# Retention and a squared-ReLU feed-forward network on one core: w_out loaded in fp32 and cast on chip, and seven products in place of eight for half of the first block

## The chip, the core and the metric

The kernel runs on one core of a Trainium2 chip. The core has a matrix engine (TensorE, PE in the profile, with its weight loads as PEld), three engines for elementwise work (VectorE or DVE, ScalarE or ACT, GpSimd or POOL) and a queue engine (SyncE or SP) that issues transfers between the memory outside and the on-chip memory. Each engine works through its own list of instructions in order and waits on semaphores for the others. TensorE writes into PSUM, in banks of 2 KB a partition, from which ScalarE or VectorE must fetch the results. The metric is the device time of one execution in microseconds; lower is better.

## What is computed

The reference is a linear attention with a decay of its own in each head, followed by a feed-forward network with squared ReLU:

```python
for t in range(S):
    state = gamma[None, :, None, None] * state + np.einsum('bhd,bhe->bhde', k[:, :, t], v[:, :, t])
    y[:, :, t] = scale * np.einsum('bhd,bhde->bhe', q[:, :, t], state)
...
x = np.ascontiguousarray(attn_out.transpose(0, 2, 1, 3)).reshape(B * S, H * D)
h = np.maximum(x @ w_in, 0.0)
return (h * h @ w_out).astype(np.float32)
```

There are 4 batches, 8 heads, 768 positions and a head size of 64, so x has 3072 rows of 512. w_in is 512 x 2048, w_out 2048 x 512. All inputs and the output are fp32; the kernel multiplies in bf16 and sums in fp32.

## The kernel before

The 3072 rows are 24 chunks of 128 tokens. Chunks are put together to blocks: the first block (block 0) has four, the other ten have two each. A chunk goes through the attention (scores within the chunk, a mask, the running state, an output y that is copied to `xt`), and a block then through the network: the first product `x @ w_in`, with the 2048 hidden units in 16 f-blocks of 128; ReLU on ScalarE (line 835) and the square on VectorE (line 806); the second product with w_out.

The order is written out by hand. After a prologue (lines 1052 to 1116) the program is a row of numbered pieces of TensorE work, made by the generator `ffn_pieces`; block 0 covers pieces 5 to 32, block 1 begins at 33. `put(place, ...)` hangs other work (a load, a cast, a part of the attention of a later chunk) behind the piece of that number, and each engine gets its instructions in the order in which the pieces and the hung work are written. `attend(m, ...)` hangs the attention of chunk m on five places: scaled q and k (line 361, VectorE) and the cast of v (line 377, POOL), the transposes with their copies on ScalarE (lines 391 to 411), two halves of scores (line 430) each with a mask on VectorE (line 437), the state (line 458), and the outputs (lines 498 and 506). The scores go through a single PSUM bank, `ps_st`, so the second half needs the first half's mask to be done. The products share four PSUM banks in the pool `ps_f`.

In block 0 pieces 5 to 16 are first products of all 512 rows at once (line 826). Pieces 17 to 32 are the second product (line 1022): for each quarter of w_out (four f-blocks), four chunks in turn, four matmuls of 512 columns each, 64 in all; the four results are copied out by ScalarE (line 1032) and stored.

Blocks 2 to 10 (`SEVEN`) do the second product otherwise. Seen as a product of 2 x 2 blocks (two chunks by even and odd f-blocks, times even and odd f-blocks by the two halves of the columns), it takes seven products of eight matmuls with 256 columns in place of eight products, in the form of Strassen and Winograd. For that VectorE makes four sums of the hidden units (s1 to s4), and once for the whole kernel four sums of w_out (t1 to t4, `sum_w_out`, line 319). Before, these are hung on places 25 (first half, four instructions), 31 (two) and 48 (two).

w_in arrives in fp32 through SP's queue into four staging tiles (pool `stage`, 4 buffers) and is cast to bf16 by VectorE, ScalarE and POOL (lines 329 to 333). w_out arrives through POOL's queue, in four quarters hung on places 6, 8, 11 and 14, and the transfer itself makes bf16 of it:

```python
nc.gpsimd.dma_start(w_out_bf[g][:], w_out_v[:, g * FPQ : (g + 1) * FPQ, :])
```

The staging tiles are used again from place 22 on by loads of k and v for later batches (line 145).

Of the kernel before, what the change touches and what calls it, by code (L numbers as in the profile page):

```python
# [9 lines left out]
FP32 = mybir.dt.float32  # L10
# [3 lines left out]
AF = mybir.ActivationFunctionType  # L14
ALU = mybir.AluOpType
# [16 lines left out]
def kernel(  # L32
# [123 lines left out]
    staged = {}  # L156
# [10 lines left out]
        staged["in", g] = t  # L167

    def load_w_out(g):
        nc.gpsimd.dma_start(w_out_bf[g][:], w_out_v[:, g * FPQ : (g + 1) * FPQ, :])  # L170

    load_q4(0)
    load_pair(0, "kn", k, raw_k, heads_of[0])
# [14 lines left out]
    def exponents(pattern, step, name, logs, parts=(slice(0, P),)):  # L188
# [35 lines left out]
        out=ident[:],  # L224
# [96 lines left out]
    def cast_w(kind, g, halves=(0, 1), on="VVSG"):  # L321

        src = staged[kind, g]
        dst = (w_in_bf if kind == "in" else w_out_bf)[g]
        for half in halves:
            c = slice(half * 256, (half + 1) * 256)
            for j, engine in enumerate(on):
                if engine == "G":
                    nc.gpsimd.tensor_copy(dst[:, j, c], src[:, j, c])
                elif engine == "V":  # L330
                    nc.vector.tensor_copy(dst[:, j, c], src[:, j, c])
                else:
                    nc.scalar.activation(dst[:, j, c], src[:, j, c], AF.Copy)

    idle_ps = []

# [503 lines left out]
    def seven_products(tb):  # L840
# [115 lines left out]

        return first_sums, rest if tb + 1 < len(BLOCKS) else rest_at_end

    open_ps = {}

    def first_unit(tb, g, c, parts=(0, 1)):

        if tb not in h2s:
            h_tiles(tb)
        if (tb, g, c) not in open_ps:
            open_ps[tb, g, c] = ps_f.tile([P, FPQ, C], FP32, name="psf")
        hp = open_ps[tb, g, c]
        cols = slice(c * C, (c + 1) * C)
        half = FPQ // 2
        for part in parts:  # L970
            for fq in range(part * half, (part + 1) * half):
                first_product(tb, hp[:, fq, :], g * FPQ + fq, cols)
        if 1 in parts:
            relu(h_of(tb, g * FPQ, (g + 1) * FPQ)[:, :, cols], open_ps.pop((tb, g, c)))

    def ffn_pieces(tb):
        nch = BLOCKS[tb]
        TB = nch * C
        if tb == 0:
            for f in range(FPQ, NFB):  # L980
                hp = ps_f.tile([P, TB], FP32, name="psf")
                first_product(tb, hp[:], f, slice(0, TB))
                relu(h_of(tb, f)[:, 0], hp)
                yield
        elif tb <= 2:

            for c in range(nch):
                for g in range(NQ):
                    first_unit(tb, g, c)
                    if tb in SEVEN and (c, g) == (1, 3):  # L990
                        first_sums, rest = seven_products(tb)
                        first_sums(slice(0, 4))
                    yield
            if tb in SEVEN:
                yield from rest()
                return
        else:
            h_tiles(tb)
            per = 512 // TB
            if tb in SEVEN:  # L1000
                first_sums, rest = seven_products(tb)
            for f0 in range(0, NFB, per):
                hp = ps_f.tile([P, per, TB], FP32, name="psf")
                for f in range(f0, f0 + per):
                    first_product(tb, hp[:, f - f0, :], f, slice(0, TB))
                relu(h_of(tb, f0, f0 + per), hp, tb in SEVEN and f0 // per in (1, 3))
                if f0 // per in (1, 2, 3) and kept:
                    next(kept[0])
                if f0 // per == 4:
                    kept.clear()  # L1010
                if f0 // per == 5 and tb in SEVEN:
                    first_sums(slice(0, 4))
                yield
            if tb in SEVEN:
                yield from rest()
                return


        def second(op, j, g, cols=slice(0, DM)):
            for fq in range(FPQ):  # L1020
                f = g * FPQ + fq
                nc.tensor.matmul(  # L1022
                    op[:],
                    lhsT=h_of(tb, f)[:, 0, j * C : (j + 1) * C],
                    rhs=w_out_bf[g][:, fq, cols],
                    start=(f == 0),
                    stop=(f == NFB - 1),
                )
# [8 lines left out]
        together = nch if tb == 0 else 1  # L1037
        for j0 in range(0, nch, together):
            ops = [ps_f.tile([P, DM], FP32, name="psf") for _ in range(together)]
            for g in range(NQ):  # L1040
                for j, op in enumerate(ops):
                    second(op, j0 + j, g)
                    if g == NQ - 1:
                        store(op, j0 + j)
                    yield


    tp, st, f = (ps_tp, "tp"), (ps_st, "st"), (ps_f, "psf")
# [75 lines left out]
    def put(place, what, *args):  # L1124
        parts.setdefault(place, []).append((what, args))
# [16 lines left out]
    def attend2(m, d, before, q_at, qturn_at, k_at, turn_at, v_at):  # L1142
# [103 lines left out]
```

## Time and profile before

| | us |
|---|---|
| median of 3 runs (204.67 to 205.03) | 204.86 |
| the profiled execution | 204.37 |
| its span on the engines | 202.5 |
| TensorE busy | 195.7 |
| VectorE busy | 151.2 |
| ScalarE busy | 127.6 |
| POOL busy | 68.0 |
| second product of block 0, first matmul to the first of block 1 | 30.92 to 47.63 |
| w_out's four loads, issue to landing | 7.1 to 13.8 |

The profile shows one execution. Times in it count from the start of the span; the execution's own time is 1.9 us longer than the span. A line of the timeline gives start, duration (of a run of like instructions, from the first's start to the last's end), engine, source line, operation, what is written from what, how many, and in brackets how long the engine stood idle before it and what ended the wait. A matmul's duration includes its way through the array, so the step between starts, not the duration, is what one costs in a row of them.

### The profile page before, as it was taken

Reading aid. Unit: us, or ns where it says so; the run is one execution under the profiler, and the core shown is the slowest. Engines: PE = TensorE matmul, PEld = TensorE weight load, DVE = VectorE, ACT = ScalarE, POOL = GpSimd, SP = SyncE. Lnnn points to the kernel's source line nnn. Section 1 sums busy time; section 2 is a strip of 40 time slices with the busy share of each in tenths; the row PEclk is TensorE's granted clock in tenths of the full one; section 3 lists DMA queues with packets and bytes.
Section 4 is the critical chain, followed back from the end, with each engine's and each line's share of the span. In section 5 each row is a group of like instructions: output and inputs, shape, how many; then the busy total and the mean of one; then the engine's idle time right before and its main releaser. Section 6 shows DMA issues by size and latency. Waiting matters only on the chain.

```text
span 202.5 us, 5744 instructions
## 1 busy us (share of the span) xinstructions
PE 195.7 (97%) x2321; PEld 160.1 (79%) x2327; DVE 151.2 (75%) x309; ACT 127.6 (63%) x258; POOL 68.0 (34%) x131
## 2 busy tenths in 40 slices
PE   5899999999999999999999999999999999999993
PEld 1478444558965998988989999999889899999883
DVE  3986768268597888788798798798797797485374
ACT  8764872348853766782784785783775776763730
POOL 8693711311330552282225225252225225100000
PEclk9999999999999999999999999999999999999999
DMA  5999999999979478979979998979998254300202
GB/s 169 356 375 398 338 195 197 260 233 320 236 160 262 125 159 156 202 204 223 171 214 164 214 208 203 226 182 227 212 157 200 107 105 49 111 3 0 107 0 104
DMA packets 92250, 38.12 MB, mean 188 GB/s; under 512 B 68544, under 2 KB 88256, under 8 KB 92224
## 3 DMA queue, kind: packets, MB, share of 16 engines
q1 hardware_dynamic: 90112, 35.66, 72.3%
q0 software_dynamic: 2112, 2.10, 6.2%
q8 instruction: 18, 0.29, 0.6%
q14 instruction: 8, 0.07, 0.1%
HBM read 27.26 MB, written 6.29 MB: 166 GB/s over the span
## 4 chain that ended last, share of the span: by engine, by line
PE 89%; DVE 4%; DMA 2%; ACT 2%; issue 1%; DVEq 0%
PE psf L826 40%; PE psf L860 18%; PE psf L1022 10%; PE tp L860 7%; DMA qn<-in_q_dram 2%; PE y L783 2%; PE st L727 2%; PE y L776 2%; PE c_ps L754 2%; DVE h L806 1%; PE c_ps L627 1%; PE st L430 1%; PE y L506 1%; ACT h L835 1%; PE y L342 1%
## 5 line engine op out<-in xcount | busy, mean ns | idle before, releaser
L826 PE MATMUL psf<-xt,w_in_bf 128*128 128x256 bf16 (+2 forms) x879 | 92.2, 259 | 0.2 <-issue 0.2
L826 PEld LDWEIGHTS <-w_in_bf 128*128 128x128 bf16 x880 | 71.2, 98 | 11.4
L835 ACT ACTIVATE h<-psf 128x512 bf16<-128x512 f32 x96 | 56.1, 594 | 20.1 <-PE psf L826 18.5
L806 DVE TENSOR_TENSOR h<-h 128x512 bf16<-128x512 bf16 x80 | 35.6, 460 | 19.2 <-ACT h L835 18.8
L688 POOL CAST ks_bdp<-stage 64x512 bf16<-64x512 f32 x32 | 24.5, 767 | 38.7 <-issue 30.7
L705 POOL COPY v_bd<-v 64x512 bf16<-64x512 bf16 x32 | 20.6, 643 | 42.0 <-DVE v L697 36.7
L860 PEld LDWEIGHTS <-h 128*128 128x128 bf16 x288 | 26.3, 98 | 3.8 <-DVE h L806 1.0
L1022 PE MATMUL psf<-w_out_bf,h 128*128 128x512 bf16 x91 | 21.9, 379 | 0.4 <-issue 0.2
L860 PE MATMUL tp<-w_out_bf,h 128*128 128x256 bf16 x136 | 19.4, 273 | 0.2 <-DVE h L806 0.2
L860 PE MATMUL psf<-w_sum,h 128*128 128x256 bf16 x136 | 19.1, 273 | 0.0
L860 PE MATMUL psf<-w_sum,k_bd 128*128 128x256 bf16 x144 | 17.9, 273 | 0.0
L361 DVE TENSOR_TENSOR qs<-qn,qf 128x512 bf16<-128x512 f32 x20 | 16.3, 824 | 0.0
L1022 PEld LDWEIGHTS <-h 128*128 128x128 bf16 x96 | 8.9, 98 | 9.0
L860 PEld LDWEIGHTS <-k_bd 128*128 128x128 bf16 x144 | 13.7, 98 | 1.5
L763 ACT ACTIVATE s_bd<-c_ps 64x256 bf16<-64x256 f32 x29 | 10.7, 370 | 6.5 <-PE c_ps L754 6.5
L856 DVE TENSOR_TENSOR osb<-psf,u 128x256 f32<-128x256 f32 x26 | 10.3, 421 | 6.1 <-PE psf L860 5.8
L856 DVE TENSOR_TENSOR u<-psf,u 128x256 f32<-128x256 f32 x18 | 7.6, 423 | 8.9 <-PE psf L860 8.7
L697 DVE TENSOR_TENSOR v<-stage,kf 128x512 bf16<-128x512 f32 x16 | 12.5, 783 | 0.0
L764 ACT ACTIVATE s_bd<-c_ps 64x256 bf16<-64x256 f32 x29 | 11.0, 378 | 0.4
L734 DVE TENSOR_TENSOR pt<-st,cmask 128x512 bf16<-128x512 f32 x16 | 11.0, 687 | 0.1
L856 DVE TENSOR_TENSOR k_bd<-h 128x512 bf16<-128x512 bf16 x18 | 10.7, 597 | 0.3
L896 ACT ACTIVATE osb<-tp 128x256 f32<-128x256 f32 x8 | 3.1, 384 | 12.2 <-PE tp L860 12.2
(133 smaller groups left out, 262.4 us busy)
## 6 DMA issues: line engine op xcount, KB each, us to landing
qn<-in_q_dram SPq DMA_DIRECT2D x12, 512.0 KB, 4.9
out_dram<-osb SPq DMA_DIRECT2D x23, 256.0 KB, 2.4
stage<-in_k_dram SPq DMA_DIRECT2D x32, 96.0 KB, 3.4
stage<-in_v_dram SPq DMA_DIRECT2D x32, 96.0 KB, 3.5
stage<-in_moe_w_in_dram SPq DMA_DIRECT2D x4, 512.0 KB, 7.1
stage<-in_moe_w_in_dram SPq DMA_DIRECT2D x2, 1024.0 KB, 10.2
w_out_bf<-in_moe_w_out_dram POOLq DMA_DIRECT2D x4, 512.0 KB, 10.3
kn<-in_k_dram SPq DMA_DIRECT2D x6, 256.0 KB, 6.0
```

The costliest lines, as they stand in the source:

```text
L361: engine.tensor_tensor(out=out, in0=by, in1=table[:, :, None].to_broadcast([P, H, D]), op=ALU.mult)
L688: nc.gpsimd.tensor_copy(ks[rows, :, hh, :].rearrange("s (u p) d -> s u p d", u=2), kn[rows])
L697: nc.vector.tensor_tensor(out=v2.rearrange("s (u p) d -> s u p d", u=2), in0=vn, in1=kf2[:, i, :, :, None].to_broadcast([P, 2, NPAIR, D]), ...
L705: nc.gpsimd.tensor_copy(v_bd[rows, :, hh, :], v2[rows])
L734: nc.vector.tensor_tensor(out=pt[:], in0=st[:], in1=cmask2.rearrange("s r t -> s (r t)")[:, None, :].to_broadcast([P, 2 * NPAIR, C // 2]), ...
L764: nc.scalar.activation(s_bd[halves[1], :, 1, :], c[halves[1]], AF.Copy)
L806: nc.vector.tensor_mul(hv, hv, hv)
L826: nc.tensor.matmul(hp, lhsT=w_in_bf[g][:, cb, fq * 128 : (fq + 1) * 128], rhs=xts[tb][:, cb, cols], start=(cb == 0), stop=(cb == NCB - 1),)
L835: nc.scalar.activation(hv, hp[:], AF.Relu)
L856: nc.vector.tensor_tensor(out=out, in0=in0, in1=in1, op=op)
L860: nc.tensor.matmul(to, lhsT=left[:, j], rhs=right(j) if callable(right) else right[:, j], start=(start and j == 0), stop=(stop and j == NF ...
L1022: nc.tensor.matmul(op[:], lhsT=h_of(tb, f)[:, 0, j * C : (j + 1) * C], rhs=w_out_bf[g][:, fq, cols], start=(f == 0), stop=(f == NFB - 1),)
```

## The change

w_out's quarters are loaded in fp32 by SP's queue into staging tiles, at places 4, 4, 6 and 10, and cast by the new function `cast_w_out` at places 14, 17, 19 and 21: the first quarter by POOL alone, the others by ScalarE and POOL in turn, one instruction of 128 x 512 for each f-block.

In block 0 the second product of chunks 0 and 1 stays as it was (32 matmuls of 512 columns). For chunks 2 and 3 it is done by seven products of eight matmuls with 256 columns, in the new function `last_of_first`. Eight steps each take two f-blocks for chunks 0 and 1 and one matmul of the first of the seven products; then come the other products. The last one is kept and issued behind the second piece of block 1. The sums of the hidden units (eight instructions of 128 x 512) are hung on places 11, 17 and 25 and use a spare tile; the four sums of w_out are needed earlier and are hung on places 23 and 25. The first places of chunk 4's attention move from 23 to 22.

```diff
     def load_w_out(g):
-        nc.gpsimd.dma_start(w_out_bf[g][:], w_out_v[:, g * FPQ : (g + 1) * FPQ, :])
+        t = stage_tile(FPQ * DM).rearrange("s (f n) -> s f n", f=FPQ)
+        nc.sync.dma_start(t, w_out_v[:, g * FPQ : (g + 1) * FPQ, :])
+        staged["out", g] = t
...
+    def cast_w_out(g, on):
+        for j, engine in enumerate(on):
+            src, dst = staged["out", g][:, j], w_out_bf[g][:, j]
+            if engine == "G":
+                nc.gpsimd.tensor_copy(dst, src)
+            else:
+                nc.scalar.activation(dst, src, AF.Copy)
...
+    def last_of_first():
...
+        def first_sums(x):
+            add(s1[x], a21[x], a22[x])
+            add(s2[x], s1[x], a11[x], ALU.subtract)
+
+        def last_sums():
+            for x in range(2):
+                add(s3[x], a11[x], a21[x], ALU.subtract)
+            for x in range(2):
+                add(s4[x], a12[x], s2[x], ALU.subtract)
+
+        def second_products():
+            ops = [ps_f.tile([P, DM], FP32, name="psf") for _ in range(2)]
+            pa, pd = (ps_f.tile([P, HN], FP32, name="psf") for _ in range(2))
...
+            for j in range(NFB // 2):
+                for f in (2 * j, 2 * j + 1):
+                    for c, op in enumerate(ops):
+                        nc.tensor.matmul(
+                            op[:],
+                            lhsT=h_of(0, f)[:, 0, c * C : (c + 1) * C],
+                            rhs=w_out_bf[f // FPQ][:, f % FPQ, :],
+                            start=(f == 0),
+                            stop=(f == NFB - 1),
+                        )
+                product(pa[:], a11, b(0, 0), (j,))
+                if j == NFB // 2 - 1:
+                    nc.scalar.activation(a[:], pa[:], AF.Copy)
+                    for c, op in enumerate(ops):
+                        osb = opool.tile([P, DM], FP32, name="osb")
+                        nc.scalar.activation(osb[:], op[:], AF.Copy)
+                        nc.sync.dma_start(out[c * C : (c + 1) * C], osb[:])
+                yield
+            lo, hi = range(0, 4), range(4, 8)
+            product(pd[:], s1, t1, lo)
+            yield
+            product(pa[:], a12, b(1, 0), lo, False)
+            yield
+            product(pa[:], a12, b(1, 0), hi, False)
+            nc.scalar.activation(oa[:, 0:HN], pa[:], AF.Copy)
+            product(pd[:], s1, t1, hi)
+            yield
+            pb, pe = (ps_f.tile([P, HN], FP32, name="psf") for _ in range(2))
+            product(pb[:], s2, t2, lo)
+            product(pb[:], s2, t2, hi)
+            add(u[:], pb[:], a[:])
+            yield
+            product(pe[:], a22, t4, lo)
+            yield
+            product(pe[:], a22, t4, hi)
+            yield
+            product(pb[:], s3, t3, lo, False)
+            yield
+            product(pb[:], s3, t3, hi, False)
+            add(v[:], pb[:], a[:])
+            add(ob[:, HN:DM], pd[:], v[:])
+            add(ob[:, 0:HN], pe[:], v[:])
+
+            def last_product():
+                product(pd[:], s4, b(1, 1), range(8), False)
+                add(oa[:, HN:DM], pd[:], u[:])
+                yield
+                nc.sync.dma_start(out[r0 + C : r0 + 2 * C], ob[:])
+                yield
+                nc.sync.dma_start(out[r0 : r0 + C], oa[:])
+                yield
+
+            kept.append(last_product())
+            yield
...
         if tb == 0:
+            first_sums, last_sums, second_products = last_of_first()
+            put(11, first_sums, 0)
+            put(17, first_sums, 1)
+            put(25, last_sums)
...
+            yield from second_products()
+            return
         elif tb <= 2:
 
             for c in range(nch):
                 for g in range(NQ):
                     first_unit(tb, g, c)
+                    if c * NQ + g in (1, 2, 3) and kept:
+                        next(kept[0])
...
+    put(4, load_w_out, 0)
+    put(4, load_w_out, 1)
     put(6, cast_w, "in", 2)
-    for g, place in enumerate((6, 8, 11, 14)):
-        put(place, load_w_out, g)
+    put(6, load_w_out, 2)
+    put(10, cast_w, "in", 3)
+    put(10, load_w_out, 3)
+    for g, place, on in ((0, 14, "GGGG"), (1, 17, "SGSG"), (2, 19, "SGSG"), (3, 21, "SGSG")):
+        put(place, cast_w_out, g, on)
...
-    put(10, cast_w, "in", 3)
-    for half, at_places in enumerate(((25, 25, 25, 25), (31, 31, 48, 48))):
+    for half, at_places in enumerate(((23, 23, 23, 23), (25, 25, 25, 25))):
         made = sum_w_out(half)
         for place in at_places:
             put(place, next, made)
-    attend(4, 21, (23, 25, 27, 29, 31))
+    attend(4, 21, (22, 25, 27, 29, 31))
```

More of the change, by code (lines that the diff above doesn't have):

```diff
@@ L957, in seven_products, with halves_of, add, product @@
         return first_sums, rest if tb + 1 < len(BLOCKS) else rest_at_end
+    def last_of_first():
+        def halves_of(k, c):
+            return [
+                t.rearrange("e (j k) (c t) -> e k c j t", k=2, c=4)[:, k, 2 + c] for t in h2s[0]
+            ]
+        (a11, a12), (a21, a22) = ([halves_of(k, c) for k in range(2)] for c in range(2))
+        n = NFB // 4
+        s1, s2, s4 = (
+            [
+                t.rearrange("e (x j t) -> e x j t", x=2, t=C)[:, x]
+                for x in range(2)
+            ]
+            for t in (spare[:, i * HN * 4 : (i + 1) * HN * 4] for i in range(3))
+        )
+        s3 = a21
+        b = lambda k, c: lambda j: w_out_bf[j // 2][:, 2 * (j % 2) + k, c * HN : (c + 1) * HN]
+        t1, t2, t3, t4 = (lambda j, t=t: t[:, j] for t in sums)
+        def add(out, in0, in1, op=ALU.add):
+            nc.vector.tensor_tensor(out=out, in0=in0, in1=in1, op=op)
+        def product(to, left, right, js, start=True, stop=True):
+            for j in js:
+                nc.tensor.matmul(
+                    to,
+                    lhsT=left[j // n][:, j % n],
+                    rhs=right(j),
+                    start=(start and j == 0),
+                    stop=(stop and j == NFB // 2 - 1),
+                    skip_group_check=True,
+                )
+        def first_sums(x):
[9 more added lines that the diff above has]
+            pa, pd = (ps_f.tile([P, HN], FP32, name="psf") for _ in range(2))
+            oa, ob = (opool.tile([P, DM], FP32, name="osb") for _ in range(2))
+            a, u, v = (upool.tile([P, HN], FP32, name=f"u{i}") for i in range(3))
+            r0 = 2 * C
+            for j in range(NFB // 2):
+                for f in (2 * j, 2 * j + 1):
+                    for c, op in enumerate(ops):
+                        nc.tensor.matmul(
+                            op[:],
[3 more added lines that the diff above has]
+                            stop=(f == NFB - 1),
+                        )
+                product(pa[:], a11, b(0, 0), (j,))
[40 more added lines that the diff above has]
+            yield
+        return first_sums, last_sums, second_products
@@ L989, in ffn_pieces @@
                     first_unit(tb, g, c)
+                    if c * NQ + g in (1, 2, 3) and kept:
+                        next(kept[0])
+                    if c * NQ + g == 4:
+                        kept.clear()
                     if tb in SEVEN and (c, g) == (1, 3):
@@ L1034, in store @@
             nc.sync.dma_start(out[r0 : r0 + C, cols], osb[:, cols])
-        together = nch if tb == 0 else 1
-        for j0 in range(0, nch, together):
-            ops = [ps_f.tile([P, DM], FP32, name="psf") for _ in range(together)]
+        for j in range(nch):
+            op = ps_f.tile([P, DM], FP32, name="psf")
             for g in range(NQ):
[L1041 to L1045, printed above, removed]
+                second(op, j, g)
+                if g == NQ - 1:
+                    store(op, j)
+                yield
     tp, st, f = (ps_tp, "tp"), (ps_st, "st"), (ps_f, "psf")
```

## The prediction

> **What bounds the kernel now.** I read the page's busy times and slices first, then the chain of waits, then the timeline from 30 to 50 us, where the change lies.
>
> ```profile
> PE 195.7 (97%) x2321; PEld 160.1 (79%) x2327; DVE 151.2 (75%) x309; ACT 127.6 (63%) x258; POOL 68.0 (34%) x131
> ...
> PEclk9999999999999999999999999999999999999999
> ...
> PE psf L826 40%; PE psf L860 18%; PE psf L1022 10%; PE tp L860 7%; DMA qn<-in_q_dram 2%; PE y L783 2%; PE st L727 2%; PE y L776 2%; PE c_ps L754 2%; DVE h L806 1%; PE c_ps L627 1%; PE st L430 1%; PE y L506 1%; ACT h L835 1%; PE y L342 1%
> ```
>
> TensorE sets the time: it is busy for 97% at the full granted clock, and it leads the chain. A matmul saved counts in full, and so does every wait put on it.
>
> ```profile
> 30.92 6.21 PE L1022 MATMUL psf<-w_out_bf,h 128*128 128x512 bf16 x27
> 32.09 1.29 DVE L361 TENSOR_TENSOR qs<-qn,qf 128x512 bf16<-128x512 f32 x2
> 33.30 0.69 DVE L361 TENSOR_TENSOR ks<-kn,kf 128x512 bf16<-128x512 f32 x1
> 33.90 0.69 DVE L319 TENSOR_TENSOR w_sum<-w_out_bf 128x1024 bf16<-128x1024 bf16 x1
> 34.62 0.69 DVE L319 TENSOR_TENSOR w_sum<-w_out_bf,w_sum 128x1024 bf16<-128x1024 bf16 x1
> 34.92 0.86 POOL L377 CAST v_bd<-vn 128x512 bf16<-128x512 f32 x1 [8.79 <-DMA vn<-in_v_dram]
> 35.23 1.10 DVE L319 TENSOR_TENSOR w_sum<-w_out_bf 128x1024 bf16<-128x1024 bf16 x1
> 36.25 0.68 DVE L319 TENSOR_TENSOR w_sum<-w_out_bf,w_sum 128x1024 bf16<-128x1024 bf16 x1
> 36.96 0.61 PE L391 MATMUL tp<-ident,qs 128*128 128x128 bf16 x8
> 39.56 1.21 ACT L411 ACTIVATE k_bd<-tp 64x512 bf16<-64x512 bf16 x2 [0.93 <-PE tp L404]
> 41.09 0.39 PE L430 MATMUL st<-qT,k_bd 128*128 128x128 bf16 x4
> 41.51 0.69 DVE L437 TENSOR_TENSOR pt<-st,cmask 128x512 bf16<-128x512 f32 x1 [4.58 <-PE st L430]
> 43.03 0.39 PE L430 MATMUL st<-qT,k_bd 128*128 128x128 bf16 x4
> ```
>
> The reader is to see three things. The second product of the first block (line 1022) starts at 30.92 without a gap. VectorE has 4.58 us of idle time until the scores' mask at 41.51, so the mask follows its matmuls at once, and the next scores, which need the same single `st` bank, never wait. And a sum that took 0.69 alone took 1.10 at 35.23, while POOL ran a cast from 34.92 to 35.78 (0.86, where the same cast takes 0.61 at 40.44): POOL's casts and VectorE's sums slow each other, by 0.41 on VectorE.
>
> **TensorE: removed and added.** 28 matmuls of 512 columns lie between 30.92 and 36.96, 0.216 each. Eight of 256 columns (line 860, starts 76.33 and 77.21) take 0.88, 0.11 each; I take half of 0.216 and a little, 0.109. Removed: 32 of 512 columns. Added: 7 x 8 = 56 of 256. The block's second product goes from 64 x 0.216 = 13.82 to 32 x 0.216 + 56 x 0.109 = 13.02: 0.81 saved if nothing waits. As a mark I use chunk 5's output products (line 498, 49.81); the last of the seven products is issued ahead of them, so the mark compares whole with whole. Without waits it would be 49.0.
>
> **Arrival of w_out.** Its four casting loads from POOL's queue go (issue 0.74 to 0.94 us each on POOL); four plain loads of 1 MB go into SP's queue behind q and k of chunk 4. The two like it in w_in:
>
> ```profile
> L164 SPq DMA_DIRECT2D stage<-in_moe_w_in_dram x2: 710/796/881, 12.0 to 12.7; - x2
> ...
> DMA to landing us min/median/max: 9.2/10.2/11.1
> ```
>
> and a stretch in which both queues ran (its last column is GB/s):
>
> ```profile
> 22.50:25.00 2.50, 2.50 (x13) 1.18 (x12) 2.26 (x8) 2.29 (x5) 2.27 (x5) 1.00 1.20 307
> ```
>
> The two landed at 21.2 and 23.8, 2.6 us for 1.05 MB, 403 GB/s. Behind 23.8 come 0.79 MB of q and k (25.8) and then w_out's quarters: 28.4, 31.0, 33.6, 36.2. In the changed program's order the fourth doesn't take w_in's last staging tile but the one of w_out's first quarter, so its issue on SP waits for POOL's four casts of that quarter: 28.4 + 4 x 0.6 = 30.8, issued by 31.7. That is before the third lands, so the transfer queue does not run dry. Behind it on SP wait the loads of chunks 4 to 7; v of chunk 4 lands near 37 instead of 34.9, and its user, chunk 4's state product, stands at 43.3.
>
> The matmul loop now takes two f-blocks at a step: 4 x 0.216 + 0.109 = 0.97, eight steps, so quarters are due at 30.9, 32.9, 34.8 and, with 0.45 for the transposes of q (36.96 to 37.41), 37.2. A cast of 128x512 takes 0.61 on POOL (line 377) and 0.60 on ScalarE (the 128x512 form of line 835). Ready: 29.0, 31.6, 34.2, 36.8. All in time, the fourth with 0.4 to spare; I cost it at nothing, and each microsecond that it is late costs one. At the 307 GB/s of the stretch above, when both queues ran, it would be 3.4 late.
>
> **VectorE.** Added here: eight sums of 128x512 bf16 (0.42 each; back to back a step is 0.35) and five of 256 columns from PSUM (0.42, step 0.35). Moved forward: two sums of w_out from 64.6 us, two from 44.6. After the last square (32.2) its queue is: two sums 0.9; qs and ks 1.8 (32.09 to 33.90); four sums of w_out 2.55 (33.90 to 36.25 less the 0.41, and one step more); four more 2.55; four sums 1.4. That is 9.2 us, ending at 41.4 (the second four, due at 37.4, find the last casts done at 36.2 + 2 x 0.6 = 37.4), and the first mask, which stands behind all of it, ends at 42.1. At the other end, six POOL casts overlap (four of w_out, two of v), 0.41 each: 43.9, mask done 44.6. I take 43.6, nearer the row at 35.23, with some casts falling beside PSUM masks (a mask took 0.68 beside a cast at 11.18, no longer than alone).
>
> The Trainium skill (SBUF — State Buffer, Who interferes with whom) says that a VectorE instruction with two SBUF inputs and a GpSimd instruction that reads SBUF exclude each other, the later one blocked for the whole of it. The row's 0.41 agrees in sign; by a whole block of 0.61 for six casts the mask would end at 45.8 and the time would be 1.2 us above the other end.
>
> **What is late next.** TensorE would reach the first scores at 30.92 + 7.78 + 0.45 + 0.44 + 0.22 + 0.44 + 0.87 = 41.1. ScalarE now has three evacuations (0.38, 0.60, 0.60; steps together 1.3) from the loop's end at 39.15 in front of k_bd (1.21): k_bd done 41.6, a wait of 0.5 that the old order (39.56 to 40.77) didn't have. The second scores are then due at 41.6 + 0.22 + 0.87 + 0.44 = 43.1 and wait for the mask: 0 to 1.5, 0.5 at 43.6. After it k_bd of chunk 5 (ScalarE, 1.2) and the next mask each hold TensorE some 0.2 to 0.4; qs (1.29), three PSUM sums and the mask of chunk 5 follow on VectorE, level with TensorE: 0.6 in all, bounds 0.4 and 0.8. Sum: -0.81 + 0.5 + 0.5 + 0.6 = +0.8; ends -0.81 + 0.5 + 0 + 0.4 = +0.1 and, with 0.5 for a late quarter, -0.81 + 0.5 + 1.5 + 0.8 + 0.5 = +2.5. Behind the mark TensorE waits for nothing over 0.2 us (its waits list), so the shift stays to the end. POOL's freed issues and the two sums gone from 64.6 give nothing: no matmul waited for them.
>
> The profiled execution took 204.37 (span 202.5 and 1.87 around it): 205.2 on its own scale. It lies 0.49 under the median 204.86, so in medians 205.7.
>
> **Rivals.**
> *VectorE keeps up.* If the mask is written before 42.7, TensorE finds `st` free, the chunk 5 masks follow at once, and only some 0.2 of ScalarE's wait is left: -0.81 + 0.2 = -0.6, 204.2. For it: 4.58 us of idle there now. Against: 7 us of work come in, 5.4 of it in front of the mask.
> *Paid back exactly.* VectorE at its early end, ScalarE's wait as worked out: +0.1, 204.9.
> *The last quarter is late.* At 307 GB/s it is cast 3.4 late; VectorE's lag hides under that, so -0.81 + 3.4 + 0.5 + 0.4 = +3.5, 208.4. For it: 0.4 of margin and an issue tied to POOL's casts. Against: the low rate is from the time of two queues, and one of them goes.
>
> **How the numbers follow.** Two times count as different from 0.2% (0.41 us) on. Forecast 0.52 (0.02 of it within 0.2%), VectorE keeps up 0.20, paid back 0.18, late quarter 0.10: faster 0.2, same 0.2, slower 0.6. The forecast's own range is 204.9 to 207.3 (the ends above). The range reaches down to 204.0 to hold the first two rivals, and leaves out most of the late quarter: 204.0 to 207.2.
>
> **What would show it.** Right: the second scores of chunk 4 (line 440 of the changed kernel) idle until DVE's mask (line 447), and before it a wait for ACT's k_bd (line 421); VectorE without idle time from 32 to 43; sums near 1.1 us where POOL casts. Wrong: a mask within 0.1 us of its scores; matmuls of line 1022 waiting for ACT or POOL casts, which makes it the late quarter; the mark before 49.4.

## The result, and the profile after

| | before | after |
|---|---|---|
| median | 204.76 us (204.56 to 205.03, 4 runs) | 207.69 us (207.51 to 207.90, 4 runs) |
| span of the profiled execution | 202.5 | 206.0 |
| first matmul of the second product | 30.92 | 31.95 |
| chunk 5's output products (the mark), first matmul | 49.87 | 53.02 |
| from the mark to the end | 152.6 | 153.0 |

The ratio is 1.0136, interval 1.011 to 1.0161: 2.9 us slower, where 0.8 was forecast and 207.2 was the upper end of the range. (The prediction's 49.81 for the mark is the weight load just ahead of that matmul.)

The page of the changed kernel still has TensorE at the top of the chain, but its busy share is down from 97% to 95%, and loads of w_out and a cast of it on POOL now stand in the chain:

```profile
PE 196.4 (95%) x2351; PEld 163.0 (79%) x2351; DVE 158.5 (77%) x322; ACT 130.5 (63%) x264; POOL 73.1 (35%) x137
...
PE psf L836 32%; PE psf L870 18%; PE tp L870 7%; DMA stage<-in_moe_w_in_dram 4%; DMA stage<-in_moe_w_out_dram 4%; PE psf L1149 3%; DMA vn<-in_v_dram 3%; SPq L164 3%; SPq L115 2%; PE st L737 2%; PE y L793 2%; PE y L786 2%; POOL w_out_bf L341 2%; PE c_ps L764 2%; DVE h L816 1%
```

TensorE's waits between 30 and 56 us (total, times, longest; the kernel before has none here):

```profile
PE st L440 <- DVE pt L447: 1.7, 2, 1.3
PE st L440 <- ACT k_bd L421: 0.4, 1, 0.4
```

Lines of the timeline of that stretch (line numbers are those of the changed kernel, where 361 became 371, 319 became 321, 411 became 421, 430 became 440 and 437 became 447):

```profile
29.01 4.68 POOL L341 CAST w_out_bf<-stage 128x512 bf16<-128x512 f32 x6 [4.03 <-DMA stage<-in_moe_w_out_dram]
...
31.95 1.03 PE L1022 MATMUL psf<-w_out_bf,h 128*128 128x512 bf16 x4
32.19 0.37 SPq L171 DMA_DIRECT2D stage<-in_moe_w_out_dram  x1
33.25 0.71 DVE L990 TENSOR_TENSOR h<-h 128x512 bf16<-128x512 bf16 x1
34.34 1.70 DVE L371 TENSOR_TENSOR qs<-qn,qf 128x512 bf16<-128x512 f32 x2
34.59 1.91 POOL L341 CAST w_out_bf<-stage 128x512 bf16<-128x512 f32 x2 [0.91 <-DMA stage<-in_moe_w_out_dram]
35.96 1.09 DVE L371 TENSOR_TENSOR ks<-kn,kf 128x512 bf16<-128x512 f32 x1
...
37.65 1.15 ACT L343 ACTIVATE w_out_bf<-stage 128x512 bf16<-128x512 f32 x2 [1.93 <-DMA stage<-in_moe_w_out_dram]
37.67 1.63 POOL L341 CAST w_out_bf<-stage 128x512 bf16<-128x512 f32 x2 [1.17 <-DMA stage<-in_moe_w_out_dram]
37.75 1.08 DVE L321 TENSOR_TENSOR w_sum<-w_out_bf,w_sum 128x1024 bf16<-128x1024 bf16 x1
...
39.37 0.95 POOL L387 CAST v_bd<-vn 128x512 bf16<-128x512 f32 x1
39.77 1.09 DVE L321 TENSOR_TENSOR w_sum<-w_out_bf,w_sum 128x1024 bf16<-128x1024 bf16 x1
...
42.35 0.23 PE L440 MATMUL st<-qT,k_bd 128*128 128x128 bf16 x1
42.97 0.34 PE L440 MATMUL st<-qT,k_bd 128*128 128x128 bf16 x3 [0.39 <-ACT k_bd L421]
43.06 0.95 POOL L387 CAST v_bd<-vn 128x512 bf16<-128x512 f32 x1
43.47 1.16 DVE L990 TENSOR_TENSOR h<-h 128x512 bf16<-128x512 bf16 x2
45.22 0.68 DVE L447 TENSOR_TENSOR pt<-st,cmask 128x512 bf16<-128x512 f32 x1
45.95 0.22 PE L440 MATMUL st<-qT,k_bd 128*128 128x128 bf16 x1 [1.33 <-DVE pt L447]
```

Three things are to be seen. VectorE is without a pause from 33.25 to the mask at 45.22, and where a POOL cast runs beside them, sums and products that take 0.43 and 0.68 alone take 0.71 and 1.09; that is 12.0 us for a queue of 9.2. The mask therefore comes over 2 us behind the first scores (42.97), and the second scores, which need the single `st` bank, wait 1.33 for it. And the fourth quarter of w_out, whose load SP issues at 32.19, is cast from 37.65 on, not from 36.2.

Here it did not hold TensorE up, but only because the second product had started 1.03 later than in the profile before. That late start lies in the prologue, where one product waits 0.8 to 1.1 us for VectorE in some executions and 0.2 in others; the change does not touch that product. That the kernel before has both starts is taken from its spans, most of which fall into two groups, of 202.4 to 202.9 and of 203.5 to 204.0; its one profile has the early start. Beside the later group the changed kernel's span of 206.0 is 2.5 us longer. Of the profiles below, e1, e3, e4, e5, e14, e15 and e16 have the early start (30.9) and e2, e6, e7, e9, e10, e11 and e13 the late one (31.95); e12 begins at 31.18, and e8 at 32.46 for a reason of its own.

### The profile page after: what moved, and what is told of

It is laid out like the page before. It is cut to its first block, busy times and chain, and to the rows that moved or that the text cites. A ratio compares the mean times of both kernels' runs of the same rounds, so it can differ in the third digit from the quotient of the medians.

```text
span 206.0 us, 5829 instructions
## 1 busy us (share of the span) xinstructions
PE 196.4 (95%) x2351; PEld 163.0 (79%) x2351; DVE 158.5 (77%) x322; ACT 130.5 (63%) x264; POOL 73.1 (35%) x137
## 4 chain that ended last, share of the span: by engine, by line
PE 70%; DMA 12%; DVE 5%; SPq 5%; POOL 2%; ACT 2%; issue 1%; DVEq 0%; POOLq 0%
PE psf L836 32%; PE psf L870 18%; PE tp L870 7%; DMA stage<-in_moe_w_in_dram 4%; DMA stage<-in_moe_w_out_dram 4%; PE psf L1149 3%; DMA vn<-in_v_dram 3%; SPq L164 3%; SPq L115 2%; PE st L737 2%; PE y L793 2%; PE y L786 2%; POOL w_out_bf L341 2%; PE c_ps L764 2%; DVE h L816 1%
## 5 line engine op out<-in xcount | busy, mean ns | idle before, releaser
L816 DVE TENSOR_TENSOR h<-h 128x512 bf16<-128x512 bf16 x80 | 37.1, 478 | 18.5 <-ACT h L845 17.9
L715 POOL COPY v_bd<-v 64x512 bf16<-64x512 bf16 x32 | 20.6, 643 | 46.5 <-DVE v L707 35.8
L698 POOL CAST ks_bdp<-stage 64x512 bf16<-64x512 f32 x32 | 23.2, 724 | 35.6 <-issue 30.7
L870 PEld LDWEIGHTS <-h 128*128 128x128 bf16 x288 | 26.3, 98 | 3.6 <-DVE h L816 0.7
L800 ACT ACTIVATE xt<-y 128x512 bf16<-128x512 f32 x16 | 9.6, 598 | 1.8 <-PE y L793 1.2
L814 ACT ACTIVATE h<-h 128x512 bf16<-128x512 bf16 x16 | 10.1, 630 | 0.5
```

Source lines behind the costliest of these rows:

```text
L698: nc.gpsimd.tensor_copy(ks[rows, :, hh, :].rearrange("s (u p) d -> s u p d", u=2), kn[rows])
L715: nc.gpsimd.tensor_copy(v_bd[rows, :, hh, :], v2[rows])
L816: nc.vector.tensor_mul(hv, hv, hv)
L870: nc.tensor.matmul(to, lhsT=left[:, j], rhs=right(j) if callable(right) else right[:, j], start=(start and j == 0), stop=(stop and j == NF ...
```

## Experiments

The kernel before was measured again beside each group of experiments: 204.98 for e1 to e4, 204.53 for e5 to e8, 204.82 for e9 to e12, 204.57 for e13 to e16. A ratio is to that time. Two theories were set against each other: the late fourth quarter of w_out, and VectorE's queue in front of the mask.

**The halves of the change (e1, e2).** e1 has the arrival and the casts alone, with the first block's product as before. e2 has the seven products alone, with w_out cast by POOL's queue as before (its edit against the changed kernel):

```diff
     def load_w_out(g):
-        t = stage_tile(FPQ * DM).rearrange("s (f n) -> s f n", f=FPQ)
-        nc.sync.dma_start(t, w_out_v[:, g * FPQ : (g + 1) * FPQ, :])
-        staged["out", g] = t
+        nc.gpsimd.dma_start(w_out_bf[g][:], w_out_v[:, g * FPQ : (g + 1) * FPQ, :])
...
-    put(4, load_w_out, 0)
-    put(4, load_w_out, 1)
     put(6, cast_w, "in", 2)
-    put(6, load_w_out, 2)
+    for g, place in enumerate((6, 8, 11, 14)):
+        put(place, load_w_out, g)
     put(10, cast_w, "in", 3)
-    put(10, load_w_out, 3)
-    for g, place, on in ((0, 14, "GGGG"), (1, 17, "SGSG"), (2, 19, "SGSG"), (3, 21, "SGSG")):
-        put(place, cast_w_out, g, on)
```

> The kernel before with w_out's new way of arriving alone (loads on SP into staging tiles, casts on POOL and ScalarE), second product and sums of w_out as before. My theory (POOL's casts and the added sums fill VectorE's queue in front of the masks): arrival alone costs nothing, since VectorE's 4.6 us of idle before the first mask takes up the slowed sums; 204.8 +-0.4, masks within 0.1 us of their scores. Rival (the arrival itself costs, or the late start of the second product at 31.95 instead of 30.92 comes from it): at least 205.7, and the second product starts near 31.9.

> The changed kernel with w_out arriving as before (casting loads on POOL's queue, places 6, 8, 11, 14), no casts on chip. The loads landed at 29.1, 32.4, 35.8 and 39.2 before; the new order wants them at 30.9, 32.9, 34.8 and 37.2. Both theories: TensorE waits some 2 us inside the loop. My theory besides: VectorE's sums run at their uncontended 0.42 and 0.69, so the wait of 1.33 for the mask goes, and the time is about 206.4 (-0.8 + 2.0 + 0.4 over 204.8). Rival (the work in front of the mask alone, not the contention): both waits add, 207.5 or more.

e1: 206.42 us, ratio 1.0070 (1.0043 to 1.0098). e2: 207.03, 1.0100 (1.0069 to 1.0132). Each half alone is slower. Lines of the timeline of e1, with the early start (30.93); this execution's span is 205.3, where six of e1's ten have 204.0 to 204.7:

```profile
39.36 1.15 ACT L343 ACTIVATE w_out_bf<-stage 128x512 bf16<-128x512 f32 x2 [3.83 <-DMA stage<-in_moe_w_out_dram]
40.42 1.00 ACT L407 ACTIVATE qT<-tp 128x1024 bf16<-128x1024 bf16 x1
41.47 0.38 PE L414 MATMUL tp<-ident,ks 128*128 128x128 bf16 x4 [1.89 <-ACT qT L407]
43.42 0.39 PE L440 MATMUL st<-qT,k_bd 128*128 128x128 bf16 x4
43.84 0.69 DVE L447 TENSOR_TENSOR pt<-st,cmask 128x512 bf16<-128x512 f32 x1 [5.75 <-PE st L440]
```

The fourth quarter lands at 39.3. The matmuls that use it are not the ones that wait: in the old order the fourth quarter is first used at 42.2 (profile of the kernel before). What waits is k's transpose, because the copy of qT stands behind the quarter's casts in ScalarE's queue. VectorE has 5.75 us of idle time before the mask. So the arrival alone costs 1.4 by the medians, and the wait that shows here is one for the load and for ScalarE's queue, not for VectorE's. In e2 (late start) a matmul of the loop waits 1.3 for POOL's load, k_bd costs 0.4 and the mask 0.3, and 207.03 lies between the two values that were expected: the mask's wait is down from 1.33, but TensorE also comes 1.3 later to it. The seven products need the last quarter of w_out five microseconds earlier than the old order does (from 37.2 instead of 42.2, counted from the early start), and in e2 it landed at 39.6.

**Taking VectorE's load away (e3, e4).** e3 casts quarters two to four on ScalarE alone; e4 puts s3 and s4 behind the masks:

```diff
-    for g, place, on in ((0, 14, "GGGG"), (1, 17, "SGSG"), (2, 19, "SGSG"), (3, 21, "SGSG")):
+    for g, place, on in ((0, 14, "GGGG"), (1, 17, "SSSS"), (2, 19, "SSSS"), (3, 21, "SSSS")):
```
```diff
-            put(25, last_sums)
+            put(29, last_sums, 3)
+            put(32, last_sums, 4)
```

> The changed kernel with the casts of w_out's second to fourth quarter all on ScalarE. My theory: six POOL casts leave the stretch of VectorE's sums, which fall to 0.42 and 0.69 each, some 2 us in all, the first mask starts near 43.3 instead of 45.2 and the wait of 1.33 goes; ScalarE is some 3 us fuller and k_bd comes 0.5 later, so 206.7, 1.0 under the changed kernel. Rival (contention is a small part, the number of sums is what matters): the mask stays above 44.5, 207.7 or more.

> The changed kernel with the four last sums of hidden units moved behind the masks (s3 to place 29, s4 to 32) and the casts left alone. My theory: 1.5 to 1.9 us less stand in front of the first mask, which starts near 43.6, and the second scores wait 0 instead of 1.33; some of it comes back at the later masks, 206.7. If the work in front of the masks is not what holds TensorE: 207.7. If the wait only moves to the products with s3 and s4: 207.5.

e3: 207.96, 1.0152 (1.0113 to 1.0190). e4: 208.88, 1.0185 (1.0147 to 1.0222). Neither is faster than the change. Lines of VectorE's timeline in e3 (start 30.92):

```profile
32.21 0.43 DVE L990 TENSOR_TENSOR h<-h 128x512 bf16<-128x512 bf16 x1
...
34.22 0.68 DVE L371 TENSOR_TENSOR ks<-kn,kf 128x512 bf16<-128x512 f32 x1
...
41.10 0.69 DVE L321 TENSOR_TENSOR w_sum<-w_out_bf 128x1024 bf16<-128x1024 bf16 x1 [3.56 <-ACT w_out_bf L343]
```

Without POOL casts beside them the sums take 0.43 and 0.68 again, which shows that the casts are what stretches them in the changed kernel. The Trainium skill (SBUF — State Buffer, Who interferes with whom) has a VectorE instruction with two SBUF inputs and a GpSimd instruction that reads SBUF exclude each other. The trace agrees in direction; the size per instruction was 0.28 to 0.41 here, less than a whole cast of 0.61. But VectorE then idles 3.56 us for the casts of the late quarter, and TensorE 2.4; e4, also with the early start, shows a wait of 1.77 for the same quarter, and then 1.08 for s3, which had been put too late. So on an early start it is the late quarter that holds these forms up, and VectorE's queue alone does not explain the loss.

e3 lost more than its wait. By stretch (length, busy times of PE, PEld, DVE, ACT, POOL, then granted clock, DMA share, GB/s):

```profile
38.00:40.00 2.00, 0.00 (x0) 0.00 (x0) 0.00 (x0) 0.61 (x2) 0.00 (x0) 1.00 0.42 97
40.00:42.00 2.00, 1.93 (x7) 0.76 (x7) 0.80 (x2) 2.00 (x5) 1.49 (x12) 0.68 0.95 215
42.00:44.00 2.00, 2.00 (x8) 0.96 (x7) 2.00 (x4) 0.79 (x3) 1.81 (x4) 0.50 1.10 286
```

After the wait the granted clock is 0.50, and a step of the loop takes 1.92 instead of 0.97. Some 1.7 us go there (3.4 us at half the clock). Two of e3's six executions have this, by their mean clock of 0.992, and took 208.67 and 209.16; the other four took 207.35 to 208.10, level with the change. So e3's median says less about the casts than its timeline does.

**The fourth quarter early (e5, e6).** In the changed kernel its load takes the staging tile of the first quarter and so waits for POOL's casts (issue at 31.8 to 32.2). e5 gives it four unused output tiles instead; e6 does the same to e1:

```diff
     def load_w_out(g):
+        if g == NQ - 1:
+            tiles = [opool.tile([P, DM], FP32, name="osb") for _ in range(FPQ)]
+            for j, t in enumerate(tiles):
+                nc.sync.dma_start(t[:], w_out_v[:, g * FPQ + j, :])
+            staged["out", g] = tiles
+            return
...
-    put(10, load_w_out, 3)
+    put(6, load_w_out, 3)
```

> The changed kernel, with w_out's fourth quarter loaded into the four output tiles that are unused at that time (four loads of 256 KB at place 6), so that its issue no longer waits for POOL's four casts of the first quarter. Nothing else differs. Late quarter (the loss comes from the fourth quarter, which landed 37.6 to 39.4 where 36.2 had been taken): the issues go by 27, the landing moves to 36.5 to 37.2 (third at 34.5 and 2.6 behind it), the casts end by 38.4, and the time falls by 0.8 to 1.5 to 206.2 to 206.9. VectorE's queue (the mask behind sums slowed by POOL's casts): the mask's wait stays near 1.3 and the time stays at 207.7, within 0.3. Transfer rate (the same bytes by the same queue, wherever they are issued): landing stays past 37.6 and the time at 207.7.

> The arrival and the casts of the change alone (the first block's product as before), with the fourth quarter loaded as in e5. Late quarter: the 1.4 that the arrival alone cost was qT of chunk 4 standing on ScalarE behind casts of a quarter that landed at 39.3; with the landing near 37 qT starts at 38.3 at the latest, the wait of the transposes of k falls from 1.9 to under 0.6, and the time to 205.0 to 205.5 beside 205.0 before. If the arrival costs by what it does to other loads or by contention with the casts, it stays at 206.2 to 206.6.

e5: 206.79, 1.0110 (1.0083 to 1.0138). e6: 205.70, 1.0039 (1.0018 to 1.0059). By the medians 0.9 and 0.7 came back, by the ratios 0.5 and 0.6: about half of what the arrival alone cost, and under a third of the whole loss. The intervals overlap those of e1 and of the change, so the sizes are rough; but every run of e5 (206.77 to 207.33) lies below every run of the change (207.51 to 207.90). In e5 the quarter's four tiles landed one after the other from 35.8 to 37.7, the last later than had been expected (36.5 to 37.2), but each can be cast as it lands; without the edit all of it landed at 37.6 in the change's profile and at 38.8 to 39.4 in e1, e3, e4 and e7. In e6 (late start) qT starts at 38.64 and k's transpose has no wait; 205.70 is still above the 205.0 to 205.5 that were expected, and what remains of its loss shows no single wait over 0.3 and stays open. e5's waits, with the early start:

```profile
PE st L447 <- DVE pt L454: 1.1, 2, 0.7
PE psf L1029 <- ACT w_out_bf L350: 0.8, 1, 0.8
PE st L447 <- ACT k_bd L428: 0.4, 1, 0.4
```

Now it is the third quarter's cast (landed at 35.1, needed at 34.8) that holds the loop, and behind it VectorE's mask again. Both theories have a share.

**Needing it later, or another queue for it (e7, e8).** e7 puts half of s1 x t1 ahead of the loop's last two steps. e8 lets POOL's queue load and cast the fourth quarter:

```diff
             for j in range(NFB // 2):
+                if j == 6:
+                    product(pd[:], s1, t1, lo)
+                    yield
```
```diff
     def load_w_out(g):
+        if g == NQ - 1:
+            nc.gpsimd.dma_start(w_out_bf[g][:], w_out_v[:, g * FPQ : (g + 1) * FPQ, :])
+            return
```

> The changed kernel, with the first half of the product s1 x t1 (four matmuls of 256 columns, 0.44) put ahead of the loop's last two steps, so that w_out's fourth quarter is needed 0.44 later; the first sum of w_out moves from place 23 to 21 for it. Late quarter: 0.3 to 0.5 less, 207.2 to 207.4. VectorE's queue: the mask is no earlier, 207.7, or later by the sum that now stands ahead of qs and ks, which k's transposes wait for, up to 208.3.

> The changed kernel, with the fourth quarter loaded and cast by POOL's queue (as all four were before), issued at place 4. Its two POOL casts and two ScalarE casts go away. Late quarter: the load runs beside the others from about 21 and lands before 36; no matmul waits for it, and the time falls by 1 to 1.8, to 205.9 to 206.7. VectorE's queue: two casts fewer beside the sums, 0.4 each, 206.9 to 207.3. If both queues share the 16 engines as in the stretch of 200 GB/s, quarters two and three come later by about 1 and it gains nothing.

e7: 207.44, 1.0133 (1.0105 to 1.0161), 0.25 below the change, which the intervals cannot tell from nothing. Its profile (late start) has the fourth quarter at 38.8, and a matmul of the loop waits 0.7 for its cast; the mask's wait is 0.3, where the changed kernel has 1.33. The quarter's lateness hides VectorE's. e8: 208.07, 1.0168 (1.0143 to 1.0193). POOL's load does not run beside the others for nothing: in e8 the first quarter lands at 31.74 instead of 28.95, the loop's first matmul waits 1.1 for its cast and starts at 32.46, and the third quarter's casts start at 36.95, where the changed kernel has them at 34.56. What POOL's load was given was taken from SP's.

**One queue at a time, then all (e9 to e12).** All on top of e5. e9: k's transposes one place earlier and the two output copies behind k_bd on ScalarE. e10: s3 and s4 behind the first mask. e11: q and k of chunk 4 loaded behind w_out's second and third quarters. e12: all of these.

```diff
-    attend(4, 21, (22, 25, 27, 29, 31))
+    attend(4, 21, (22, 24, 27, 29, 31))
```
```diff
-            put(25, last_sums)
+            put(27, last_sums, True)
+            put(33, last_sums, False)
```

> e5 (the changed kernel with the early fourth quarter, 206.8), with the transposes of k of chunk 4 at place 24 instead of 25 and the two output copies of chunks 0 and 1 on ScalarE behind k_bd instead of ahead of it. Three queues, each taken to bind: ScalarE: the waits for k_bd of chunk 4 (0.66 in e5) go and the time falls by 0.5 to 0.7, to 206.1 to 206.3. VectorE: its queue ends at the same time, the mask stays at 44.4 to 44.5, TensorE only comes to that wait earlier, and the time stays at 206.8 within 0.2.

> e5, with the sums s3 and s4 behind the first mask: s3 at place 27, s4 at 33. VectorE: the first mask comes at 43.1 instead of 44.46, s4 (0.74) leaves the queue ahead of ks and mask of chunk 5, and the time falls by 0.5 to 0.9, to 205.9 to 206.3. If only the arrival counts (e5's wait of 0.81 for the third quarter's cast), nothing changes: 206.8.

> e5, with q of chunk 4 loaded behind w_out's second quarter and k of chunk 4 behind the third, instead of both ahead of the first. Arrival: the third quarter lands at 33.5 to 34.3 instead of 35.1, the wait of 0.81 goes, and the time falls by 0.6 to 0.8, to 206.0 to 206.2. VectorE: the wait only moves to the mask, 206.7 to 206.9.

> The edits of e5, e9, e10 and e11 together. If the three queues each hide the next (VectorE first), e9 and e11 give nothing alone and this gives more than the sum of the three: 205.2 to 205.8. If the three are independent, the gains add up: 206.8 less what e9, e10 and e11 each gave. Under 204.5 it would beat the kernel before.

e9: 207.10, 1.0098 (1.0064 to 1.0131). e10: 207.71, 1.0130 (1.0103 to 1.0157). e11: 206.91, 1.0096 (1.0062 to 1.0129). e12: 207.24, 1.0112 (1.0082 to 1.0142). None gains on e5's 206.79 by the medians; by the ratios e9 and e11 lie 0.2 to 0.3 us below it, well inside the intervals. e9 has only one kind of wait left (start 31.95):

```profile
PE st L447 <- DVE pt L454: 2.2, 2, 1.8
```

k_bd's 0.4 is gone and the mask's wait has grown by what was saved, from 1.33 in the changed kernel to 1.83 at the same start. That is what the expectation gave for VectorE as the bound. e11's profile (late start) has no wait for any cast, 0.4 for k_bd, and 1.1 for the first mask; since a late start by itself spares the cast's wait, it does not show what the new order of loads did. In e10 (late start) the first mask comes at 43.39 and costs nothing, but s4 had been put too far back (e12 has the same wait, and 0.8 for a POOL cast of the fourth quarter); the two lines are VectorE's s4 and the last of the seven products:

```profile
51.92 0.75 DVE L997 TENSOR_TENSOR h<-h,h 128x512 bf16<-128x512 bf16 x2
...
52.40 1.05 PE L1001 MATMUL psf<-w_out_bf,h 128*128 128x256 bf16 x8 [1.25 <-DVE h L997]
```

**The order that the waits ask for (e13 to e16).** e13 is e10 with s4 at place 31. e14 adds e9's edit. e15 moves chunk 5's scores one place back. e16 makes the edits of e15 on e2, where nothing is cast on chip, with POOL's loads at places 4, 5, 7 and 9.

```diff
-            put(33, last_sums, False)
+            put(31, last_sums, False)
...
-    attend(5, None, (28, 30, 31, 32, 34))
+    attend(5, None, (28, 30, 32, 33, 34))
```

> e10 with s4 at place 31 instead of 33; VectorE idled 1.07 there in e10 (46.73 to 47.79), and two sums of s4 take 0.74. VectorE's queue: the wait of the last product for s4 (1.25) goes, no other takes its place, and the time falls from 207.7 to 206.3 to 206.6, below e5's 206.8. If the queue has no room, a wait of 0.5 or more shows at chunk 5's mask and the time stays over 206.8.

> e13 and e9's edit on ScalarE together. e9 alone gave nothing, since the mask took over its wait. With the mask early, ScalarE's order: 0.4 to 0.7 below e13, 205.7 to 206.1. If VectorE still binds (its sums end at 43.4 in e10, TensorE's second scores at 44.3), 0.2 at most.

> e14 with the scores of chunk 5 one place later (32 and 33 instead of 31 and 32), behind the last half of s3 x t3 and behind a unit of the next block. Waits in order: the 0.32 for k_bd and the 0.5 for the mask of chunk 5 go, 0.5 to 0.8 less than e14, 205.0 to 205.5; this is what is left of the loss beside the third quarter's cast (0.8). If the outputs of chunk 5 then wait for their mask, nothing is gained.

> e2 (the seven products with w_out loaded and cast by POOL's queue, as before the change) with the edits of e9, e13 and e15, and the four loads at places 4, 5, 7 and 9 instead of 6, 8, 11 and 14. No casts run beside VectorE's sums, so they take 0.69 each, not 1.09. If the casts and the arrival are what is left, no matmul waits over 0.3 from the second product to the mark: the saving of 0.8 shows, 203.8 to 204.4, below the kernel before. If POOL's queue can't bring the last quarter by 37, its wait of 1.3 in e2 stays, and the time is 205.3 to 205.8.

e13: 206.80, 1.0102 (1.0080 to 1.0125). e14: 206.58, 1.0101 (1.0074 to 1.0129). e15: 208.82, 1.0193 (1.0143 to 1.0243). e16: 208.28, 1.0182 (1.0134 to 1.0230). e13 takes 0.9 off e10 (0.6 by the ratios), but ends level with e5: the 1.25 us for s4 are gone, and a wait of 0.5 for a ReLU on ScalarE has come in. e14 (early start) is the fastest form of the change by the medians, and what it still waits for is spread over ScalarE (a cast and a ReLU) and VectorE (a mask and the scaled k):

```profile
PE psf L1029 <- ACT w_out_bf L350: 0.8, 1, 0.8
PE psf L843 <- ACT h L852: 0.5, 1, 0.5
PE st L447 <- DVE pt L454: 0.3, 1, 0.3
PE tp L421 <- DVE ks L378: 0.3, 1, 0.3
```

e15 was to free 0.5 to 0.8 at chunk 5's scores. Lines of its VectorE and TensorE (early start):

```profile
45.98 1.71 DVE L378 TENSOR_TENSOR qs<-qn,qf 128x512 bf16<-128x512 f32 x2
47.62 0.74 DVE L997 TENSOR_TENSOR h<-h,h 128x512 bf16<-128x512 bf16 x2
...
48.85 0.76 DVE L997 TENSOR_TENSOR osb<-psf,u 128x256 f32<-128x256 f32 x2
49.52 0.68 DVE L454 TENSOR_TENSOR pt<-st,cmask 128x512 bf16<-128x512 f32 x1
```
```profile
47.28 1.05 PE L843 MATMUL psf<-xt,w_in_bf 128*128 128x128 bf16 x16
...
50.26 0.38 PE L447 MATMUL st<-qT,k_bd 128*128 128x128 bf16 x4 [1.92 <-DVE pt L454]
...
51.18 1.91 PE L843 MATMUL psf<-xt,w_in_bf 128*128 128x128 bf16 x16
```

One place further back, the mask of chunk 5 falls behind q of chunk 6, s4 and three sums from PSUM, 3.5 us of VectorE's work (45.98 to 49.52). TensorE waits 1.92, and after it the same 16 matmuls take 1.91 instead of 1.05. The one execution of e15 with a mean clock of 1.0 (0.992 in the other three) took 207.51, still over e14. e16 has the same wait and the same halved clock, and beside them 0.9 and 0.4 for w_out from POOL's queue, so it does not tell whether the casts as such cost anything; its two executions with a mean clock of 1.0 took 207.53 and 207.55. No form that was tried is as fast as the kernel before.

## Why the prediction was wrong

Its direction was right, and so was the mechanism for VectorE and ScalarE, with the list of what to look for: the second scores behind VectorE's mask, a wait for k_bd before it, VectorE without idle time, sums near 1.1 beside POOL's casts. The sizes by its own terms, in the profiled execution (starts of matmuls, waits as the gaps between a step's end and the next start):

| term | forecast | measured |
|---|---|---|
| matmuls saved | -0.81 | -0.79 (32 x 0.2155 less 56 x 0.109) |
| ScalarE, k_bd of chunk 4 | 0.5 | 0.67 |
| VectorE, first mask | 0.5 (0 to 1.5) | 1.49 |
| chunk 5's k_bd and mask | 0.6 (0.4 to 0.8) | 0.6 (0.32 + 0.51, less 0.23 that the kernel before had) |
| sum | +0.8 | +2.0, and +2.1 by the mark (21.07 less 18.95) |
| the fourth quarter of w_out | nothing | 0.5 to 0.9 (e5 against the change, e6 against e1) |

Two steps failed. In the profiled execution the second is the larger, 1.0 of the 1.3 us by which the mark missed; the first does not show there as a wait, because the quarter landed at 37.6 and the second product had started late. The first is "All in time, the fourth with 0.4 to spare; I cost it at nothing". The issue at 31.7 was nearly right (31.8 to 32.2: POOL's four casts of the first quarter took 0.8 to 0.9 each, not 0.6). The landing at 36.2 was not: where the load is issued then (the change, e1, e3, e4, e7), it took 5.4 to 7.6 us from its issue, and landed at 37.6 to 39.4. The estimate took 403 GB/s for the whole stretch. The change reached that from 26 to 32 us, but while q and k of chunk 4 were coming in between w_in and w_out, the rate was 200 to 277 GB/s (24 to 26 us). In the change k of chunk 4, the load ahead of w_out, landed at 26.3 instead of 25.8, which uses up the margin by itself (in the profile of the kernel before it had landed at 26.2), and the third quarter landed at 34.3 to 34.5 instead of 33.6. Nor does it hold that "the transfer queue does not run dry": from 33 to 34 us, just behind the late issue, 225 to 318 GB/s moved, and 406 in e5, which issues the load early. With 0.4 of margin at the end of 12 us of loads in a row, the prediction should have cost the lateness at some tenths at least. It also missed what stands behind a late cast: it named who waits for SP's queue, but not that qT stands behind the last casts on ScalarE, which is the whole wait of 1.9 in e1.

The second is the size of the mask's wait. The step named the price of a cast beside a sum rightly (0.41), but took 43.6, less than four collisions, "with some casts falling beside PSUM masks". None did. Six casts (two of the third quarter, two of the fourth, two of v), as many as it had counted, each stretched an instruction of VectorE by about 0.4, and a seventh instruction (33.25, by 0.28) met the last cast of the second quarter, which ran until 33.7 because the six casts from 29.01 on took 4.68 instead of 3.66. That is 2.7 us on the queue, where 1.5 had been taken and 2.5 was the end.

The far end of the prediction's own sum was +2.5, and the medians are 2.9 apart: the terms together were too small, and not only their middle values. The two terms are not simply added: a late quarter hides some of VectorE's lag (e7), and with the quarter early VectorE's lag shows again (e5). The rival "the last quarter is late" had this mechanism and was given 10%, with a price of 3.4 for the quarter and VectorE's lag lying under it. Where the quarter did hold TensorE up, that is what the profiles show (2.4 in e3, 1.8 in e4 and 0.7 in e7, with 0.3 for the mask in each); but it cost less than 3.4, and in the change's own profile it is the mask that is waited for. Of the rest, some 0.35 lies behind the mark without a wait that the profile names; with the 2.1 before the mark it makes up the 2.5 by which the changed kernel's profile is longer than the later group of the kernel before. How far the late start adds to the four runs of the change, which all lie within 0.4, was not settled: the early and the late starts are 0.6 to 0.7 apart in e5 and e9, and cannot be told apart in the change's own runs.

## What to carry to other kernels

A product that needs fewer matmuls also needs its inputs sooner and its helpers' work in less time; before counting its saving, draw up for each queue (loads, casts, copies, sums) when it delivers and when the shorter product is due. Where three queues stand within half a microsecond of the same due time, freeing one moves the wait to the next: here the best of the re-orderings regained 1.1 of 2.9 by the medians, 0.7 by the ratios, and the intervals still overlap. And in an engine's in-order queue, ask of a late arrival not only who uses it, but what else is queued behind its cast.

## What the runs showed of the hardware

- A pause of TensorE can cost nearly its length again. After 2.4 us of waiting in e3, and after 1.92 in e15 and e16, the granted clock was 0.50 for 3.4 us, and in e15 16 matmuls took 1.91 instead of 1.05; after waits of 1.89 (e1), 1.83 (e9) and 1.77 (e4) nothing of the kind shows. Whether the length of the pause decides, or where it falls, these runs do not tell. The Trainium skill (TensorE: Matmul & The Clock Gate, What's actually happening) has the clock halve after an idle window of about 3.4 us. The halving agrees; the idle time that was enough here, 1.92 us, is shorter.
- The same load of 1 MB on the same queue took 5.4 us from issue to landing in one execution and 7.6 in another, with some 70 to 100 GB/s moving in the last two microseconds (38 to 40 us in e1 and e3). What the last packets waited for is not in the trace.
- The prologue has two lengths, 1.03 us apart: of the profiles of the change and its variants, each of one execution, eight show the longer, and the spans of the kernel before, with the same prologue, fall into two groups as far apart.
